# Attention by pairs of query tiles from the first tile on, and a weight conversion without a clamp

## The chip, the core and the metric

The kernel runs on one core of a Trainium2 chip. The metric is the device time of one execution in microseconds (us). The engines are TensorE (PE, with its weight loads as PEld), VectorE (DVE), ScalarE (ACT), GpSimd (POOL) and SyncE (SP), which issues most DMAs. Each engine takes its instructions in the order in which the program gives them, so an instruction that waits holds up everything behind it on its engine.

## What is computed

```python
# 1. local attention: B=4, H=8, S=768, D=64; chunks of 32 queries see 16 keys to
#    the left, 8 to the right, and 8 memory keys
scores = scale * q_c @ k_full.T              # per head and chunk
a = exp(scores - max); a = a / (sum(a) + 1e-9)
out[chunk] = a @ v_full
x = out.transpose(0, 2, 1, 3).reshape(3072, 512)
# 2. gated MLP, weights 512 x 1536 and 1536 x 512, given as float64
g = x @ w_gate
x = (g * sigmoid(g) * (x @ w_val)) @ w_out
# 3. mixture of experts: each token goes to the argmax of 8 experts
out = gate_w * sigmoid(x @ w_output_gate)[e] * (relu(x @ w1[e]) @ w2[e])
```

Queries, keys and values are float32. Products run in a split form: each operand is a high part plus a low part, and three products (high-high, high-low, low-high) are summed.

## The kernel before, in words

**Stages.** The 3072 tokens are eight groups of 384. The attention of group 0 runs first by itself (here "the front"). Then the gated MLP of group 0 runs column by column: the 1536 hidden columns are 12 blocks `f` of 128, and for each block TensorE makes a gate product, a value product and an output product. Between these products the attention of group 1 is fed in, then group 2's while group 1's MLP runs, and so on (`slot` calls `run_pieces`, which issues entries of the list `pieces`). The third stage comes after group 7 and isn't touched here. The order on all engines is that of the Python code, with no scheduler behind it.

**Attention tiles.** A tile is 64 queries (two chunks) of all 8 heads, with 96 keys. `at_T` transposes queries and keys on TensorE; one transpose of queries serves two tiles. For tiles 0 to 13 (`PAIRED` is 14) the queries of a tile are copied into a block-diagonal tile `qbd`: two heads share the 128 rows of the array, each against zeros in the other's half. `at_S` then adds the mask as a product (`identb` times `masks`), makes four products of 128x128 weights, takes the maximum on VectorE and the exponentials on ScalarE. From tile 14 on, `at_S2` makes the scores of two tiles at once from plain queries: sixteen products of 64 rows by 64 columns, four for each pair of heads, each in another quarter of the array. The mask is then added on VectorE (`at_X`). `at_N` divides by the sums (GpSimd up to tile 11), `at_PT` transposes the probabilities, `at_PV` and `at_PV2` multiply them with the values (one tile, two tiles) and split the result into `xh` and `xl`.

**Weights.** While the front and group 0 run, the MLP's weights are converted from float64 in 36 steps of 128x512: `load_w` fetches into one of six staging buffers, `conv_act` starts on ScalarE, `conv_dve` goes on with three VectorE instructions and an addition on GpSimd, and `conv_rest` then asks for a further load. Seven steps are spread over the front, the rest one to a slot. `split_gv` and `split_o` split a block's weights: the high part on ScalarE, the low part on GpSimd. All of this shares the PSUM pool `ps_a` of three buffers with the transposes, the PV products and, from group 1 on, the scores. `LOADS` is the order of the first transfers (w: a weight block, q: queries with their keys, v: values).

Of the kernel before, what the change touches and what calls it, by code (L numbers as in the profile page):

```python
# [21 lines left out]
def tile_chunk_attention_moe_moe2(  # L22
# [324 lines left out]
    def at_S(i, pt=None):  # L347
        t = i % NT
        mi = 1 if t == 0 else (2 if t == NT - 1 else 0)
        mk = masks[:, mi:mi + 1, :].to_broadcast([P, HP, CTXM])  # L350
        fast = i < 15
        qT, kT = qkT[i, 0], qkT[i, 1]
        ps = start_psum(i, ps_o, "o", [P, HP, CTXM])
        if fast:
            nc.tensor.matmul(ps, identb, mk, start=True, stop=False)
        between = iter(()) if pt is None else pt_steps(pt)
        for j in range(HP):
            nc.tensor.matmul(
                ps[:, j, :], qT[:, j, :], kT[:, j, :],
                start=not fast, stop=not fast or j == HP - 1)  # L360
            next(between, None)
        next(between, None)
# [8 lines left out]
        for j in range(HP):  # L371
            nc.scalar.activation(
                out=s[:, j, :], in_=src[:, j, :], func=AF.Exp,
                bias=mx[:, j, :], accum_out=den[:, j, 0:1])
        probs[i] = (s, den)

    def at_S2(i):
        qT = qkT.pop((i, 0))
        kT = [qkT.pop((i + u, 1)) for u in range(2)]
        ps = [ps_a.tile([P, HP, CTXM], F32, tag="a", name="ps_att") for z in range(2)]  # L380
        for j in range(HP):
            for z, u in ((0, 0), (1, 1), (0, 1), (1, 0)):
                d, c = slice(z * D, z * D + D), slice(u * QT, u * QT + QT)
                nc.tensor.matmul(  # L384
                    ps[z][c, j, :], qT[d, j, c], kT[u][d, j, :], start=True, stop=True)
        for z in range(2):
            score[i + z] = ps[z]

    def at_X(i):
        t = i % NT // 2 * 2  # L390
        mi = 3 if t == 0 else (4 if t == NT - 2 else 0)
        mk = masks[:, mi:mi + 1, :].to_broadcast([P, HP, CTXM])
        s = ap2.tile([P, HP, CTXM], F32, tag="s", name="s", bufs=3)
        mx = sm.tile([P, HP, 1], F32, tag="mx", name="mx")
        nc.vector.tensor_tensor(out=s, in0=score.pop(i), in1=mk, op=ALU.add)
        nc.vector.tensor_reduce(out=mx, in_=s, axis=AX.X, op=ALU.max, negate=True)  # L396
        den = dens[i % 3]
        for j in range(HP):
            nc.scalar.activation(  # L399
                out=s[:, j, :], in_=s[:, j, :], func=AF.Exp,  # L400
# [24 lines left out]

    def at_PV(i):
        g, tt = divmod(i, GU)
        if g not in xT:
            xT[g] = (xp.tile([P, KD, GT], F32R, tag="xh", name="xh"),
                     xp.tile([P, KD, GT], F32R, tag="xl", name="xl"))  # L430
        xh, xl = xT[g]
        vt = vals.pop(i)
        u = i % 2
        ps = ps_a.tile([P, HP, QT], F32, tag="a", name="ps_pv")
# [884 lines left out]
```

## Time and profile before

| | us |
|---|---|
| median of 3 runs (lowest to highest) | 1111.65 (1111.19 to 1112.65) |
| the profiled execution's own time | 1112.31 |
| its span, from first to last instruction | 1110.5 |
| busy: PE, PEld | 1075.1 (97%), 966.2 (87%) |
| busy: DVE, ACT, POOL | 585.0 (53%), 594.6 (54%), 630.5 (57%) |
| DMA | 125.73 MB, mean 113 GB/s |

The span leaves 1.8 us of the execution outside it. The shares are means over stages that differ: TensorE is busy nearly all the time after the first 140 us, while VectorE and GpSimd have most of their load in those first 140 us.

### The profile page before, as it was taken

The page shows a single profiled execution, that of the slowest core. Times are in us where ns is not written, and L with a number is a line of the kernel's source. Part 1 is how long each engine was busy: PE and PEld are TensorE (multiplying, and loading weights), DVE is VectorE, ACT ScalarE, POOL GpSimd, SP SyncE. Part 2 cuts the span into 40 slices and gives each one's busy share as a digit, 9 for nine tenths or more (in the row PEclk, how much of TensorE's full clock was granted, in tenths as well). Part 3 has the DMA queues.
Part 4 walks back from the last instruction along what each step waited for, and adds up shares of the span by engine and source line. Part 5 has one row for each costly group of instructions (what it writes and reads, how often), then busy time and mean ns, then how long its engine had stood idle before and what let it go on. Part 6 is the DMA issues. An engine that isn't in the chain of part 4 may idle for free.

```text
span 1110.5 us, 20227 instructions
## 1 busy us (share of the span) xinstructions
PE 1075.1 (97%) x7268; PEld 966.2 (87%) x7268; DVE 585.0 (53%) x1260; ACT 594.6 (54%) x1318; POOL 630.5 (57%) x438
## 2 busy tenths in 40 slices
PE   7899999999999999999999999999999999999994
PEld 5788898998999999899999899899889988888883
DVE  6799944444534543544454353534785444444563
ACT  5588845555555555555555554435544434445551
POOL 4599954654554465564455456565214456667782
PEclk7799999999999999999999999999999999999997
DMA  8887524211211211211121000255329755565774
GB/s 216 211 233 210 140 61 115 67 39 38 59 32 39 68 40 24 56 37 39 39 63 36 22 31 7 89 92 166 126 57 342 242 172 183 181 188 189 223 233 127
DMA packets 204574, 125.73 MB, mean 113 GB/s; under 512 B 110768, under 2 KB 181552, under 8 KB 204466
## 3 DMA queue, kind: packets, MB, share of 16 engines
q1 hardware_dynamic: 199282, 110.70, 36.4%
q0 software_dynamic: 5184, 13.66, 3.6%
q8 instruction: 59, 0.97, 0.4%
q14 instruction: 49, 0.40, 0.1%
HBM read 110.82 MB, written 14.04 MB: 112 GB/s over the span
## 4 chain that ended last, share of the span: by engine, by line
PE 81%; DVE 11%; issue 3%; POOL 2%; ACT 1%; DMA 1%; SPq 0%; POOLq 0%; ACTq 0%; DVEq 0%
PE ps_g L562 32%; PE acc L603 16%; PE g L1071 11%; PE o L1106 11%; PE ps_pv L459 2%; PE ps_t L326 2%; DVE ps_c L229 2%; DVE w L232 2%; DVE ps_c L227 2%; PE ps_att L420 2%; PE ps_att L384 1%; PE ps_x L651 1%; PE a L1057 1%; POOL gvl L184 1%; PE ps_l L659 1%
## 5 line engine op out<-in xcount | busy, mean ns | idle before, releaser
L184 POOL TENSOR_TENSOR gvl<-w,gvh 128x1024 fp32r<-128x1024 f32 x96 | 230.4, 2401 | 98.8 <-ACT gvh L183 97.2
L562 PE MATMUL ps_g<-xh,gvh 128*128 128x384 f32 x768 | 268.5, 350 | 0.6 <-ACT gvh L183 0.6
L562 PE MATMUL ps_g<-xh,gvl 128*128 128x384 f32 x768 | 259.5, 338 | 0.4 <-POOL gvl L184 0.4
L562 PE MATMUL ps_g<-xl,gvh 128*128 128x384 f32 x768 | 259.3, 338 | 0.0
L184 POOL TENSOR_TENSOR ol<-w,oh 128x512 fp32r<-128x512 f32 x96 | 125.6, 1309 | 181.8 <-ACT oh L183 151.8
L603 PE MATMUL acc<-oh,h 128*128 128x512 f32 x576 | 201.0, 403 | 0.0
L575 DVE SCALAR_TENSOR_TENSOR th<-th,ps_g 128x384 f32<-128x384 f32 x96 | 53.1, 553 | 202.8 <-ACT th L570 202.8
L562 PEld LDWEIGHTS ps_g<-xh,gvh 128*128 128x128 f32 x768 | 145.0, 189 | 4.1 <-ACT gvh L183 0.8
L562 PEld LDWEIGHTS ps_g<-xl,gvh 128*128 128x128 f32 x768 | 145.2, 189 | 2.0
L562 PEld LDWEIGHTS ps_g<-xh,gvl 128*128 128x128 f32 x768 | 144.9, 189 | 0.8 <-POOL gvl L184 0.8
L586 ACT CAST h<-th 128x384 fp32r<-128x384 f32 x96 | 49.1, 512 | 155.3 <-DVE th L584 155.3
L603 PEld LDWEIGHTS acc<-oh,h 128*128 128x128 f32 x576 | 108.2, 188 | 26.5 <-issue 3.8
L603 PE MATMUL acc<-ol,h 128*128 128x512 f32 x288 | 113.7, 395 | 0.3 <-POOL ol L184 0.3
L1081 ACT ACTIVATE h<-g 128x256 fp32r<-128x256 f32 (+2 forms) x96 | 36.1, 376 | 141.4 <-PE g L1071 123.4
L183 ACT CAST gvh<-w 128x1024 fp32r<-128x1024 f32 x96 | 100.4, 1047 | 1.6 <-POOL w L235 1.6
L570 ACT ACTIVATE th<-ps_g 128x384 f32<-128x384 f32 x96 | 47.2, 491 | 81.9 <-PE ps_g L562 79.3
L1083 DVE SCALAR_TENSOR_TENSOR h<-g,h 128x256 fp32r<-128x256 f32 (+2 forms) x96 | 39.3, 410 | 94.8 <-ACT hc L1081 41.8
L584 DVE TENSOR_TENSOR th<-th,ps_g 128x384 f32<-128x384 f32 x96 | 53.1, 553 | 68.3 <-PE ps_g L562 66.9
L592 DVE TENSOR_TENSOR h<-th,h 128x384 fp32r<-128x384 f32 x96 | 64.1, 668 | 31.2 <-ACT h L586 31.2
L1106 PE MATMUL o<-wh,h 128*128 128x512 f32 x184 | 65.8, 396 | 0.9 <-DVE h L1083 0.9
L1106 PE MATMUL o<-gvh,h 128*128 128x512 f32 x184 | 66.1, 398 | 0.5 <-DVE h L1083 0.5
L399 ACT ACTIVATE s<-s,mx 128x96 f32<-128x96 f32 x136 | 49.4, 364 | 32.0 <-DVE mx L396 31.9
(254 smaller groups left out, 2275.1 us busy)
## 6 DMA issues: line engine op xcount, KB each, us to landing
w<-in_moe_w_dram SPq DMA_DIRECT2D x120, 256.0 KB
ra<-in_moe_w_dram SPq DMA_DIRECT2D x72, 256.0 KB
kt<-in_k_dram SPq DMA_DIRECT2D x35, 176.0 KB
vt<-in_v_dram SPq DMA_DIRECT2D x35, 176.0 KB
xs<-xr SPq DMA_DIRECT2D x8, 769.5 KB
st<-in_moe_w_gate_dram SPq DMA_DIRECT2D x12, 512.0 KB
st<-in_moe_w_val_dram SPq DMA_DIRECT2D x12, 512.0 KB
st<-in_moe_w_out_dram SPq DMA_DIRECT2D x12, 512.0 KB
```

The costliest lines, as they stand in the source:

```text
L183: nc.scalar.copy(out=hi, in_=src)
L184: lo_eng.tensor_tensor(out=lo, in0=src, in1=hi.bitcast(F32), op=ALU.subtract)
L399: nc.scalar.activation(out=s[:, j, :], in_=s[:, j, :], func=AF.Exp, bias=mx[:, j, :], accum_out=den[:, j, 0:1])
L562: nc.tensor.matmul(ps, a[:, c], x[:, kk, :], start=(n == 0), stop=(n == 3 * KD - 1))
L570: nc.scalar.activation(out=th, in_=ps, func=AF.Tanh, scale=0.5)
L575: nc.vector.scalar_tensor_tensor(out=th, in0=th, scalar=1.0, in1=ps, op0=ALU.add, op1=ALU.mult)
L584: nc.vector.tensor_tensor(out=hh, in0=hh, in1=ps, op=ALU.mult)
L586: nc.scalar.copy(out=h1, in_=hh)
L592: nc.vector.tensor_tensor(out=h2, in0=hh, in1=h1.bitcast(F32), op=ALU.subtract)
L603: nc.tensor.matmul(accs[g][j], a[:, c], w_, start=(f == 0 and n == 0), stop=(f == NF - 1 and n == 2))
L1071: nc.tensor.matmul(ps, wx[:, 0, c * P:(c + 1) * P], xx[:, c, :], start=(i == 0), stop=(i == 3 * KD - 1))
L1106: nc.tensor.matmul(ysd[s][t][0:hx.shape[1]], hx, wx[:, 1], start=(j == 0 and i == 0), stop=(j == NFE - 1 and i == len(passes) - 1))
```

## The change

- Scores go by pairs (`at_S2`) from tile 0 on; `at_S`, `at_PV` and the block-diagonal tiles `qbd` are gone, with their two GpSimd memsets. Queries are copied by one ScalarE instruction for a pair; before it was two, on VectorE in the front and on ScalarE behind it. In the front the mask stays a product; from tile 6 on it is added on VectorE (before: from tile 15 on).
- The pieces of the front are written out by hand in a new order, and `LOADS` with them: queries and keys of four tiles come ahead of most weights and values.
- The conversion loses its first VectorE instruction (the clamp): ScalarE's existing pass multiplies the high word by 2^-112, which moves the exponent as the clamp and the mask did together.
- While group 0 runs, the low part of the output weights (`ol`) is made on VectorE and no more on GpSimd.

```diff
-    LOADS = "w0 q0 q1 q2 w1 v0 v1 q3 w2 q4 w3 w4 v2 w5 q5 v3 v4 v5"
+    LOADS = "q0 q1 w0 q2 q3 w1 v0 v1 w2 q4 q5 w3 v2 v3 w4 v4 v5 w5"
...
-        nc.scalar.activation(out=ps, in_=hi.bitcast(F32), func=AF.Abs)
+        nc.scalar.activation(out=ps, in_=hi.bitcast(F32), func=AF.Abs, scale=REBIAS)
...
         nc.vector.tensor_scalar(
-            out=ps, in0=ps, scalar1=MINF, scalar2=MAXF, op0=ALU.max, op1=ALU.min)
-        nc.vector.tensor_scalar(
-            out=pi, in0=pi, scalar1=3, scalar2=0x3FFFFFFF,
+            out=pi, in0=pi, scalar1=3, scalar2=0x7FFFFFFF,
             op0=ALU.logical_shift_left, op1=ALU.bitwise_and)
...
-    def split_o(f):
+    def split_o(f, lo_eng):
...
-            pair = qbd[i // 2 % 2]
...
+            t = ap2.tile([P, HP, P], F32, tag="qT", name="qT")
+            copy_out(False, t, ps, SCALE)
+            qkT[i, 0] = t
             return
-        t = ap2.tile([P, HP, CTXM], F32, tag="kT", name="kT")
+        t = ap2.tile([P, HP, CTXM], F32, tag="kT", name="kT", bufs=4)
...
+    def at_S2(i):
+        qT = qkT.pop((i, 0))
+        kT = [qkT.pop((i + u, 1)) for u in range(2)]
+        ps = [start_psum(i, ps_o, "o", [P, HP, CTXM]) for z in range(2)]
+        fast = i < GU
         if fast:
-            nc.tensor.matmul(ps, identb, mk, start=True, stop=False)
...
+            mk = pair_mask(i)
+            for z in range(2):
+                nc.tensor.matmul(ps[z], identb, mk, start=True, stop=False)
         for j in range(HP):
...
+            for z, u in ((0, 0), (1, 1), (0, 1), (1, 0)):
+                d, c = slice(z * D, z * D + D), slice(u * QT, u * QT + QT)
+                nc.tensor.matmul(
+                    ps[z][c, j, :], qT[d, j, c], kT[u][d, j, :],
+                    start=not fast, stop=not fast or j == HP - 1)
...
+        yield from convert(0)
         yield at_T, (0, 0)
         yield at_T, (0, 1)
...
+        yield at_T, (1, 1)
+        yield at_S2, (0,)
+        yield at_X, (0,)
+        yield at_T, (2, 0)
+        yield at_T, (2, 1)
+        yield at_X, (1,)
+        yield from convert(1)
+        yield at_N, (0,)
+        yield at_T, (3, 1)
+        yield at_N, (1,)
+        yield at_S2, (2,)
...
+        yield at_X, (4,)
+        yield from convert(4)
+        yield at_PT, (2,)
+        yield at_X, (5,)
+        yield at_PT, (3,)
+        yield from convert(5)
+        yield at_N, (4,)
+        yield at_PV2, (2,)
+        yield at_N, (5,)
+        yield from convert(6)
+        yield at_PT, (4,)
+        yield at_PT, (5,)
+        yield at_PV2, (4,)
...
-                split_o(f)
+                split_o(f, nc.vector if late else nc.gpsimd)
```

**VectorE, the first MLP column of group 0.** Before, from the gate's `th` on (line 575): three instructions to a conversion (L227 is the clamp), with a copy of keys (`kT`), the value's product (L584) and the low part of `h` (L592) between them.

```order
L575 SCALAR_TENSOR_TENSOR th<-th,ps_g 128x384
L227 TENSOR_SCALAR ps_c<-ps_c 128x512
L229 TENSOR_SCALAR ps_c<-ps_c 128x512
L232 SCALAR_TENSOR_TENSOR w<-st,ps_c 128x512
L584 TENSOR_TENSOR th<-th,ps_g 128x384
L315 COPY kT<-ps_t 128x384
L227 TENSOR_SCALAR ps_c<-ps_c 128x512
L229 TENSOR_SCALAR ps_c<-ps_c 128x512
L232 SCALAR_TENSOR_TENSOR w<-st,ps_c 128x512
L592 TENSOR_TENSOR h_665<-th,h_644 128x384
L369 TENSOR_REDUCE mx<-ps_att 128x4
L227 TENSOR_SCALAR ps_c<-ps_c 128x512
```

In the changed program the same stretch, from its line 527 on:

```order
L527 SCALAR_TENSOR_TENSOR th<-th,ps_g 128x384
L178 TENSOR_TENSOR ol<-w,oh 128x512
L307 COPY kT<-ps_t 128x384
L221 TENSOR_SCALAR ps_c<-ps_c 128x512
L224 SCALAR_TENSOR_TENSOR w<-st,ps_c 128x512
L536 TENSOR_TENSOR th<-th,ps_g 128x384
L307 COPY kT<-ps_t 128x384
L221 TENSOR_SCALAR ps_c<-ps_c 128x512
L224 SCALAR_TENSOR_TENSOR w<-st,ps_c 128x512
L544 TENSOR_TENSOR h_667<-th,h_647 128x384
L221 TENSOR_SCALAR ps_c<-ps_c 128x512
L224 SCALAR_TENSOR_TENSOR w<-st,ps_c 128x512
```

A conversion has two instructions, and `ol`, which was GpSimd's, stands behind the gate's `th` in every column.

**VectorE, where a pair of PV products is copied out in group 0.** Before, with the tile's `xh` and `xl`:

```order
L575 SCALAR_TENSOR_TENSOR th<-th,ps_g 128x384
L315 CAST xh<-ps_pv 128x4x128
L468 TENSOR_TENSOR xl<-ps_pv,xh 128x4x128
L227 TENSOR_SCALAR ps_c<-ps_c 128x512
L229 TENSOR_SCALAR ps_c<-ps_c 128x512
L232 SCALAR_TENSOR_TENSOR w<-st,ps_c 128x512
L584 TENSOR_TENSOR th<-th,ps_g 128x384
```

After:

```order
L178 TENSOR_TENSOR ol<-w,oh 128x512
L307 CAST xh<-ps_pv 128x4x128
L407 TENSOR_TENSOR xl<-ps_pv,xh 128x4x128
L360 TENSOR_TENSOR s<-ps_att,masks 128x384
L362 TENSOR_REDUCE mx<-s 128x4
L221 TENSOR_SCALAR ps_c<-ps_c 128x512
L224 SCALAR_TENSOR_TENSOR w<-st,ps_c 128x512
```

Behind `xl` now come the mask addition (L360) and maximum (L362) of the next pair's scores, whose products TensorE makes after the PV products; `ol` stands in front.

**ScalarE, the start of the front.** Before, from the first conversion step (L218, L219); L372 are the four exponentials of a tile, L423 copies transposed probabilities:

```order
L218 ACTIVATE ps_c<-st 128x512
L219 ACTIVATE st<-st 128x512
L372 ACTIVATE s,den_104<-ps_att,mx 128x96 x4
L218 ACTIVATE ps_c<-st 128x512
L219 ACTIVATE st<-st 128x512
L372 ACTIVATE s,den_105<-ps_att,mx 128x96 x4
L218 ACTIVATE ps_c<-st 128x512
L219 ACTIVATE st<-st 128x512
L423 COPY pT<-ps_att 96x512
L372 ACTIVATE s,den_106<-ps_att,mx 128x96 x4
```

After, where L365 are the exponentials and L305 copies the queries of a pair:

```order
L212 ACTIVATE ps_c<-st 128x512
L213 ACTIVATE st<-st 128x512
L305 ACTIVATE qT<-ps_t 128x512
L365 ACTIVATE s,den_104<-ps_att,mx 128x96 x4
L305 ACTIVATE qT<-ps_t 128x512
L365 ACTIVATE s,den_105<-ps_att,mx 128x96 x4
L212 ACTIVATE ps_c<-st 128x512
L213 ACTIVATE st<-st 128x512
L365 ACTIVATE s,den_106<-ps_att,mx 128x96 x4
L212 ACTIVATE ps_c<-st 128x512
```

The queries' copies have come to ScalarE, the first of them behind the conversion of w0, and the exponentials of tiles 0 and 1 now stand ahead of the second conversion.

## Rows read from the trace of the kernel before

**Rows 1.** Windows (us, then busy PE, PEld, DVE, ACT, POOL, clock, DMA, GB/s).

```profile
47.40:134.00 86.60, 79.06 (x514) 69.90 (x513) 82.90 (x145) 73.15 (x169) 78.07 (x57) 1.00 0.74 206
134.00:154.70 20.70, 20.70 (x141) 19.15 (x141) 12.12 (x21) 9.86 (x24) 13.06 (x9) 1.00 0.21 53
154.70:245.70 91.00, 89.82 (x673) 82.22 (x673) 40.63 (x89) 50.00 (x121) 47.31 (x27) 1.00 0.29 72
```

**Rows 2.** Timeline of VectorE from 47.36 us: start, duration, instruction.

```profile
47.36 0.56 DVE L315 COPY kT<-ps_t 128x384 f32<-128x384 f32 x1 [6.10 <-PE ps_t L326]
47.84 0.69 DVE L227 TENSOR_SCALAR ps_c<-ps_c 128x512 f32<-128x512 f32 x1
48.56 0.70 DVE L229 TENSOR_SCALAR ps_c<-ps_c 128x512 int32<-128x512 int32 x1
49.29 0.69 DVE L232 SCALAR_TENSOR_TENSOR w<-st,ps_c 128x512 int32<-128x512 int32 x1
49.90 0.55 DVE L575 SCALAR_TENSOR_TENSOR th<-th,ps_g 128x384 f32<-128x384 f32 x1
```

**Rows 3.** Groups by line, 47.4 to 134: busy us, mean ns.

```profile
L227 DVE TENSOR_SCALAR ps_c<-ps_c 128x512 f32<-128x512 f32 x29 | 19.9, 686 | 0.0
...
L592 DVE TENSOR_TENSOR h<-th,h 128x384 fp32r<-128x384 f32 x9 | 6.0, 662 | 0.0
```

**Rows 4.** Timeline of VectorE: the end of group 0.

```profile
154.72 0.69 DVE L632 TENSOR_SCALAR xr<-acc 128x512 f32<-128x512 f32 x1 [0.40 <-PE acc L603]
```

**Rows 5.** Timeline of TensorE: scores of one tile at 61.07, of two at 351.11.

```profile
61.07 0.34 PE L355 MATMUL ps_att<-masks,identb 128*128 128x384 bf16 x1
...
62.05 0.42 PE L562 MATMUL ps_g<-xh,gvh 128*128 128x384 f32 x1
...
351.11 0.89 PE L384 MATMUL ps_att<-kT,qbd 64*64 64x96 f32 x32
351.93 0.50 PE L603 MATMUL acc<-oh,h 128*128 128x512 f32 x1
```

**Rows 6.** The mask addition on VectorE: ns min/median/max.

```profile
L395 DVE TENSOR_TENSOR s<-ps_att,masks x34: 545/548/551, 167.4 to 663.5; 128x384 f32<-128x384 f32 x34
```

**Rows 7.** Low parts made on VectorE in the third stage: ns min/median/max.

```profile
L1007 DVE TENSOR_TENSOR gvl<-w,gvh x36: 669/691/2756, 789.1 to 1068.0; 128x512 fp32r<-128x512 f32 x36
L1007 DVE TENSOR_TENSOR wl<-w,wh x36: 669/691/1360, 796.6 to 1072.8; 128x512 fp32r<-128x512 f32 x36
```

**Rows 8.** Timeline of the front, SP and ScalarE.

```profile
0.81 0.44 SPq L204 DMA_DIRECT2D st<-in_moe_w_gate_dram  x1
...
4.85 0.63 ACT L218 ACTIVATE ps_c<-st 128x512 f32<-128x512 f32 x1 [2.44 <-DMA st<-in_moe_w_gate_dram]
...
5.41 0.64 ACT L219 ACTIVATE st<-st 128x512 int32<-128x512 uint32 x1
...
10.86 0.34 ACT L372 ACTIVATE s<-ps_att,mx 128x96 f32<-128x96 f32 x1 [4.81 <-DVE mx L369]
```

**Rows 9.** Timeline of the end of the front.

```profile
36.39 0.83 POOL L410 TENSOR_TENSOR s<-s,rec 128x384 f32<-128x384 f32 x1 [1.24 <-ACT ps_c L218]
...
37.27 1.09 PE L420 MATMUL ps_att<-ident,s 128*96 128x128 f32 x4 [1.22 <-POOL s L410]
...
38.37 1.97 PE L437 MATMUL ps_pv<-pT,first 96*64 96x64 f32 x32
38.40 0.58 ACT L423 COPY pT<-ps_att 96x512 f32<-96x512 f32 x1 [1.10 <-PE ps_att L420]
...
40.01 4.67 POOL L184 TENSOR_TENSOR gvl<-w,gvh 128x1024 fp32r<-128x1024 f32 x2 [0.36 <-ACT gvh L183]
...
42.41 0.69 PE L562 MATMUL ps_g<-xh,gvl 128*128 128x384 f32 x1 [0.41 <-POOL gvl L184]
...
46.02 0.49 ACT L570 ACTIVATE th<-ps_g 128x384 f32<-128x384 f32 x1 [5.15 <-PE ps_g L562]
```

**Rows 10.** The chain of waits: the exponentials of tile 0.

```profile
10.86 1.41 ACT s L372 x8
```

**Rows 11.** Windows of the front.

```profile
10.00:38.40 28.40, 23.91 (x165) 20.16 (x164) 24.35 (x52) 17.66 (x66) 14.54 (x27) 0.62 0.93 239
38.40:46.70 8.30, 7.28 (x49) 6.52 (x50) 2.29 (x6) 2.96 (x4) 5.91 (x3) 0.50 0.78 194
```

**Rows 12.** Timeline of TensorE: a pair of PV products in group 0.

```profile
119.76 1.15 PE L459 MATMUL ps_pv<-pT,vt 96*64 96x64 f32 x32 [0.31 <-ACT kT L317]
```

**Rows 13.** The chain of waits: one product of a column, 134 to 160.

```profile
136.56 2.11 PE ps_g L562 x12
138.66 2.10 PE acc L603 x9
```

More of the change, by code (lines that the diff above doesn't have):

```diff
@@ L345, in at_T, with pair_mask, at_X @@
         qkT[i, 1] = t
[L347 to L353, printed above, removed]
+    def pair_mask(i):
+        t = i % NT // 2 * 2
+        mi = 3 if t == 0 else (4 if t == NT - 2 else 0)
+        return masks[:, mi:mi + 1, :].to_broadcast([P, HP, CTXM])
+    def at_S2(i):
[3 more added lines that the diff above has]
+        fast = i < GU
         if fast:
-            nc.tensor.matmul(ps, identb, mk, start=True, stop=False)
-        between = iter(()) if pt is None else pt_steps(pt)
+            mk = pair_mask(i)
+            for z in range(2):
+                nc.tensor.matmul(ps[z], identb, mk, start=True, stop=False)
         for j in range(HP):
[L358 to L362, printed above, removed]
+            for z, u in ((0, 0), (1, 1), (0, 1), (1, 0)):
[3 more added lines that the diff above has]
+                    start=not fast, stop=not fast or j == HP - 1)
+        for z in range(2):
+            score[i + z] = ps[z]
+    def at_X(i):
         s = ap2.tile([P, HP, CTXM], F32, tag="s", name="s", bufs=3)
         mx = sm.tile([P, HP, 1], F32, tag="mx", name="mx")
-        src = ps
-        if not fast:
-            nc.vector.tensor_tensor(out=s, in0=src, in1=mk, op=ALU.add)
+        src = score.pop(i)
+        if i >= GU:
+            nc.vector.tensor_tensor(out=s, in0=src, in1=pair_mask(i), op=ALU.add)
             src = s
@@ L373, in at_S @@
                 out=s[:, j, :], in_=src[:, j, :], func=AF.Exp,
[L374 to L400, printed above, removed]
                 bias=mx[:, j, :], accum_out=den[:, j, 0:1])
@@ L412, in at_PT @@
     def at_PT(i):
-        for _ in pt_steps(i):
-            pass
-    def pt_steps(i):
         p = probs.pop(i)[0]
@@ L424, in pt_steps @@
         pT[i] = t
[L426 to L434, printed above, removed]
-        for h in range(H):
-            z = h % 2
-            nc.tensor.matmul(
-                ps[z * D:z * D + D, h // 2, :], vt[:, h, :],
-                pT[i][:, h // 2, z * QT:z * QT + QT] if i < PAIRED
-                else pT[i - u + z][:, h // 2, u * QT:u * QT + QT],
-                start=True, stop=True)
-        dst = (slice(None), slice(None), slice(tt * QT, (tt + 1) * QT))
-        if i + 3 >= GU:
-            load_v(i + 3)
-        copy_out(i < 2 * GU, xh[dst], ps)
-        nc.vector.tensor_tensor(out=xl[dst], in0=ps, in1=xh[dst].bitcast(F32), op=ALU.subtract)
     def at_PV2(i):
@@ new lines, in attention_pieces @@
+        yield at_S2, (0,)
[8 more added lines that the diff above has]
+        yield at_S2, (2,)
+        yield at_X, (2,)
+        yield from convert(2)
+        yield at_PT, (0,)
+        yield at_T, (4, 0)
+        yield at_X, (3,)
+        yield at_PT, (1,)
+        yield at_T, (4, 1)
+        yield from convert(3)
+        yield at_N, (2,)
@@ L501, in attention_pieces @@
+        yield at_T, (5, 1)
+        yield at_PV2, (0,)
+        yield at_N, (3,)
+        yield at_S2, (4,)
+        yield at_X, (4,)
[11 more added lines that the diff above has]
+        yield at_PV2, (4,)
         yield at_T, (GU, 0)
         yield at_T, (GU, 1)
-        for n in range(GU, PAIRED):
-            yield at_T, (n + 1, 0)
-            yield at_T, (n + 1, 1)
-            if n % 2 == 0 and n - 4 >= GU:
-                yield at_PV2, (n - 4,)
-            yield at_S, (n,)
-            if n - 2 >= GU:
-                yield at_PT, (n - 2,)
-            if n - 1 >= GU:
-                yield at_N, (n - 1,)
@@ L513, in attention_pieces @@
[L513 to L519 removed]
+        yield at_T, (GU + 1, 1)
+        for n in range(GU, NTT + 2, 2):
+            if n > GU:
                 yield at_PT, (n - 2,)
@@ L1147, in tile_chunk_attention_moe_moe2 @@
                 load_w(*divmod(z, 3))
-        run_pieces(12)
+        run_pieces(pieces.index((at_S2, (2,))))
         setup_routing()
```

77 lines of the change are left out of this document (21 added, 56 removed).

## Prediction

> **What bounds the kernel now.** I first looked where the change lies: the front, and group 0 of the MLP, up to the copy of group 0's sums at 154.72 us [rows 4]. Behind that point the code of groups 1 to 7 and of the third stage is the same, apart from an order of pieces that group 2 had already. Group 1 took 91.0 us with TensorE busy for 89.8 of it at the full clock [rows 1], so nothing off TensorE matters there.
>
> The windows split the beginning in three. From 47.4 to 134 us VectorE is busy 82.9 of 86.6 us; TensorE (79.1), GpSimd (78.1) and ScalarE (73.2) come behind it [rows 1]. The reader is to see in the timeline [rows 2] that VectorE's instructions stand without a gap, one starting as the last one ends: copy, clamp, shift, merge, silu. From 134 to 154.7 TensorE is busy all the time [rows 1]: the conversions are over. So VectorE sets the time from 47.4 to 134, TensorE after that.
>
> Ahead of 47.4 lies the front. There VectorE is busy 24.4 of 28.4 us between 10 and 38.4, TensorE 23.9, at a mean clock of 0.62 [rows 11]; it is a chain of latencies that VectorE paces. It ends with the last copy of probabilities on ScalarE (38.40, 0.58 long), the split of the first weights on GpSimd (40.01) and TensorE going on at 42.41 behind it [rows 9]. VectorE then has nothing to do until 47.36, 6.1 us [rows 2].
>
> **The change part by part, group 0.** The sum is made against the profiled execution's 1112.3 us, which is 0.66 above the median.
>
> *The clamp.* It takes 686 ns, 29 times in the stretch [rows 3]; from its start to the next instruction's it is 0.72 us (47.84 to 48.56) [rows 2]. 29 x 0.72 = 20.9 us come off VectorE. ScalarE's pass stays the same instruction with a factor; I price that at nothing.
>
> *The idle time before 47.36.* VectorE waits there for a copy of keys whose transposes stand behind the first gate product. In the new order only queries come at that place, and they go to ScalarE. The seventh conversion's two instructions (0.73 + 0.61, [rows 2]) therefore run in the gap: -1.3 us.
>
> *`ol` on VectorE.* The same operation and shape stands in the third stage: median 0.69 us, but up to 2.76 [rows 7]. In the stretch the low part of `h`, also a subtraction of two SBUF tiles, has a mean of 662 ns for 384 columns [rows 3], where a 384-column instruction that reads PSUM takes 0.55 [rows 2, 6]. So there is some waiting beside a busy GpSimd. I take 0.76 for each of the 10 that fall in the stretch: +7.6 us; bounds 0.6 and 2.76. The Trainium skill, "GPSIMD Engine Reference" (Specifications), states that GpSimd's SBUF interface is shared with VectorE and contended by VectorE instructions with two SBUF inputs. The trace agrees: the long ones are of that kind. By that rule an edit that adds ten such instructions beside GpSimd costs more than their bare 0.69 us, or 6.9 in all.
>
> *The mask on VectorE.* Eight tiles (6 to 13) at 548 ns [rows 6], 0.48 from start to start, as for the copy of keys, which is of that size (47.36 to 47.84, [rows 2]): +3.8 us.
>
> *Waits that come with the pairs.* `at_S2` takes two buffers of `ps_a`, which has three; one is held by the conversion in flight and one by the PV products just made. So the second half of the scores waits until `xl` is copied out on VectorE, and VectorE's next instruction is the mask addition of these same scores. It stands idle for the sixteen products, 0.82 us [rows 5], and some 0.1 of handover, four times: +3.6. Lower bound 0; upper bound 2.5 each, if VectorE also waits for the PV products (1.15 us, [rows 12]) with its queue empty.
>
> *What costs nothing here.* On TensorE a tile took 0.98 us for mask and scores (61.07 to 62.05), a pair will take 0.82 [rows 5]: 4 x (1.96 - 0.82) = 4.6 us less, which hides behind VectorE as long as VectorE is the bound. GpSimd loses ten `ol`, and ScalarE four copies of queries; neither ended a wait that counts. If VectorE stops being the bound, TensorE is next (rival B).
>
> **The front.** Now the chain is longer, as pairs wait for both tiles. Its steps at 1.2 GHz, in which most of the front ran:
> - Start. w0 landed 4.04 us after its request at 0.81 [rows 8]. Now q0 and the keys of two tiles (0.6 MB) are ahead of its 0.5 MB, which at 239 GB/s [rows 11] moves its landing to about 7.4 us (estimate: 0.8, 1.9 of start-up, 4.7 of transfer). ScalarE, in order, then converts (1.2, two passes, [rows 8]), copies the queries (0.6); the second tile's keys get their PSUM buffer only then: transposes 0.9, copy 0.6, scores 1.6 (double of 0.82), maximum 0.6. The exponentials of tile 0 start at 12.9; before, at 10.86.
> - To the exponentials of tile 2: VectorE has keys, maximum, conversion, sums, keys (4.6), then scores 1.6 and a maximum: 6.8.
> - To those of tile 4: ScalarE has two tiles' exponentials (1.41 each, [rows 10]), a conversion, two copies of probabilities and one of queries (5.8); then PV products 1.97 [rows 9], two masks 1.1, scores and maximum: 11.0.
> - To the last copy of probabilities: 5.2 of ScalarE, then PV 2.0, `xh` and `xl` 1.3, the sums 0.3, the division 0.83, the transposes 1.09, the copy 0.58 [rows 9]: 11.3, since the division of tile 5 stands behind the copies of the PV products.
>
> That is 42.0 us. With TensorE's pieces halved it would be 35.9. At the mean clock of 0.62 (a quarter of the time at 2.4 GHz) it is 40.5, against 38.98 before: +1.5. Bounds -3.1 and +3.0. The conversions' clamps and the block-diagonal copies that leave the front are inside these steps: they no longer set it.
>
> **Sum.** -20.9 - 1.3 + 7.6 + 3.8 + 3.6 + 1.5 = -5.7: 1106.6 for the profiled execution, 1106.0 against the median.
>
> **The rivals.**
> - *B: TensorE becomes the bound of group 0.* The waits of the pairs vanish in VectorE's reserves and nothing holds TensorE. Its floor: group 1's 91.0, two further products of 2.1 [rows 13] (the gate and value of group 1's first column lie ahead of the copy), 1.8 for the first product at the half clock [rows 11], some 2 for the first pair of group 1: 99 from 42.41, so 141.4 instead of 154.7. With the front's 1.5 that is -11.8: 1100. For it: VectorE's sum falls below TensorE's. Against it: VectorE, TensorE, ScalarE and GpSimd would all be above four fifths busy, each in order.
> - *C: the gain is given back.* The four pairs cost 2.0 each (+4.4), and the front stays at 1.2 GHz throughout (+1.5): 1111.9, no difference. For it: the front spends most of its time at that clock already [rows 11].
> - *D: slower.* GpSimd holds VectorE up at every `ol`. The price decides: without `ol` the sum is -13.3, so it is even at 1.33 us each and slower by over 0.2% at 1.55. At 2.0 it is +6.7: 1118. For it: the maxima of 1.36 and 2.76 [rows 7]. Against it: the medians of 0.69 in a stage where GpSimd does the same subtractions.
>
> **How the numbers follow.** Main case 0.60, with a range of its own from 1102 to 1109.5 (waits from nothing to 1.8 each, the front from -2 to +2.5). B 0.16, C 0.16, D 0.08. The likeliest gives 1106. 0.2%, about what a measurement of this kernel can tell from no change, is 2.2 us: 1109.4 to 1113.9. The main case lies almost wholly below that, so faster 0.76, same 0.16, slower 0.08. From 1099.5 to 1111.5 is left out less than half of B and C and all of D, under 2 in 10.
>
> **What the profile after would show.** The clamp right: two instructions to a conversion, 1.34 us from start to start. Group 0: its sums copied near 149 (154.72 less 5.7); VectorE still densest between 47 and 130, with gaps of about 0.9 at each mask addition that follows `xl`. `ol` near 0.76 in the mean. The front: the exponentials of tile 0 near 12.9, the last copy of probabilities near 40. From there to the end the same 956 us as before; if these differ, I have overlooked something in the later groups. The prediction is wrong if the mean of `ol` passes 1.3, if TensorE rather than VectorE is without gaps in group 0, or if the front ends more than 3 us from where I put it.

## The result, and the profile after

The changed kernel takes 1122.3 us (1121.6 to 1122.6), the kernel before 1112.15 in the same comparison: ratio 1.0091, 95% interval 1.0077 to 1.0105. It is 10 us slower, where 1106.0 was forecast with a range up to 1111.5: the forecast was wrong in its sign. The profiled execution took 1122.49.

Timeline of VectorE in the kernel after, the ends of groups 0 and 1:

```profile
165.71 0.69 DVE L584 TENSOR_SCALAR xr<-acc 128x512 f32<-128x512 f32 x1
...
256.37 0.69 DVE L584 TENSOR_SCALAR xr<-acc 128x512 f32<-128x512 f32 x1 [0.84 <-PE acc L555]
```

Group 0 ends at 165.71 where it ended at 154.72 [rows 4]: +11.0, the whole loss. From there to the end the profiled executions take 956.8 us, and 957.6 before. Windows of the kernel after (columns as in [rows 1]):

```profile
10.00:38.40 28.40, 20.09 (x214) 15.84 (x214) 15.59 (x35) 18.28 (x67) 13.52 (x25) 0.68 0.96 239
50.00:130.00 80.00, 66.84 (x468) 57.29 (x467) 63.40 (x110) 56.11 (x133) 54.49 (x39) 0.91 0.69 192
165.70:256.40 90.70, 90.70 (x681) 82.81 (x681) 40.50 (x90) 51.05 (x124) 47.64 (x27) 1.00 0.30 79
```

And of the kernel before, in the middle stretch:

```profile
50.00:130.00 80.00, 73.82 (x482) 65.48 (x483) 77.22 (x136) 67.74 (x159) 74.07 (x55) 1.00 0.75 213
```

The columns after the length of a window are the busy time of PE, PEld, DVE, ACT and POOL. Every engine got emptier: VectorE fell from 77 to 63 of 80 us, but TensorE from 74 to 67 as well, and its mean granted clock from 1.00 to 0.91. No engine is nearly full any more; they wait for one another. The waits of VectorE from 46 to 165 us say where (engine, what waits, for what: us in all, times, longest):

```profile
DVE ol L178 <- ACT oh L177: 11.3, 10, 1.6
DVE th L527 <- ACT th L522: 8.6, 9, 3.0
DVE s L360 <- PE ps_att L349: 3.5, 2, 1.7
```

The first can't occur in the kernel before, where `ol` is GpSimd's, and it was not in the forecast. One of the ten, in VectorE's timeline:

```profile
85.82 0.56 DVE L527 SCALAR_TENSOR_TENSOR th<-th,ps_g 128x384 f32<-128x384 f32 x1 [0.40 <-ACT th L522]
88.01 1.63 DVE L178 TENSOR_TENSOR ol<-w,oh 128x512 fp32r<-128x512 f32 x1 [1.64 <-ACT oh L177]
89.57 0.68 DVE L307 CAST xh<-ps_pv 128x512 fp32r<-128x512 f32 x1
90.28 0.69 DVE L407 TENSOR_TENSOR xl<-ps_pv,xh 128x512 fp32r<-128x512 f32 x1
92.69 0.56 DVE L360 TENSOR_TENSOR s<-ps_att,masks 128x384 f32<-128x384 f32 x1 [1.73 <-PE ps_att L349]
93.29 0.55 DVE L362 TENSOR_REDUCE mx<-s 128x4 f32<-128x384 f32 x1
```

in ScalarE's at the same time:

```profile
85.69 0.58 ACT L305 ACTIVATE qT<-ps_t 128x512 f32<-128x512 f32 x1
86.16 0.65 ACT L212 ACTIVATE ps_c<-st 128x512 f32<-128x512 f32 x1
86.75 0.67 ACT L213 ACTIVATE st<-st 128x512 int32<-128x512 uint32 x1
87.32 0.60 ACT L177 CAST oh<-w 128x512 fp32r<-128x512 f32 x1
93.88 0.38 ACT L365 ACTIVATE s<-s,mx 128x96 f32<-128x96 f32 x1 [5.95 <-DVE mx L362]
```

and in TensorE's, with a window of the 2 us behind its wait:

```profile
91.11 1.55 PE L349 MATMUL ps_att<-kT,qT 64*64 64x96 f32 x30 [3.61 <-DVE xl L407]
```

```profile
91.10:93.20 2.10, 2.09 (x32) 1.78 (x33) 0.51 (x1) 0.00 (x0) 0.00 (x0) 0.50 1.04 255
```

VectorE reaches `ol` and stands 1.64 us, since ScalarE has a copy of queries and a conversion ahead of `oh`. Then `ol` takes 1.63. Behind it stand `xh` and `xl`. The second half of the pair's scores on TensorE waits 3.61 us for `xl` and then runs at a granted clock of 0.50, the lower level (1.2 GHz). The mask and the maximum wait for these scores, and the exponentials for the maximum; ScalarE, with its next conversion behind them, is idle 5.95 us.

**What `ol` takes.** Groups by line from 49.4 to 150 us in the kernel after (busy us, mean ns | idle ahead):

```profile
L178 DVE TENSOR_TENSOR ol<-w,oh 128x512 fp32r<-128x512 f32 x11 | 13.2, 1202 | 12.8 <-ACT oh L177 11.3 <-issue 1.5
```

These `ol` take 1.20 us in the mean, not 0.76. Four of them in VectorE's timeline,

```profile
52.10 0.69 DVE L178 TENSOR_TENSOR ol<-w,oh 128x512 fp32r<-128x512 f32 x1 [1.60 <-ACT oh L177]
...
60.29 1.10 DVE L178 TENSOR_TENSOR ol<-w,oh 128x512 fp32r<-128x512 f32 x1 [1.18 <-ACT oh L177]
...
88.01 1.63 DVE L178 TENSOR_TENSOR ol<-w,oh 128x512 fp32r<-128x512 f32 x1 [1.64 <-ACT oh L177]
...
119.47 1.64 DVE L178 TENSOR_TENSOR ol<-w,oh 128x512 fp32r<-128x512 f32 x1 [1.64 <-ACT oh L177]
```

and what GpSimd does at the times of the last three (at 52.10 it does nothing):

```profile
58.46 2.39 POOL L178 TENSOR_TENSOR gvl<-w,gvh 128x1024 fp32r<-128x1024 f32 x1
60.80 1.76 POOL L227 TENSOR_TENSOR w<-w,st 128x512 int32<-128x512 int32 x1
...
87.82 1.28 POOL L227 TENSOR_TENSOR w<-w,st 128x512 int32<-128x512 int32 x1
...
119.27 1.28 POOL L227 TENSOR_TENSOR w<-w,st 128x512 int32<-128x512 int32 x1
```

With GpSimd idle, `ol` takes 0.69 us. GpSimd's instructions end at 60.85, 89.10 and 120.55; the three `ol` end 0.54, 0.54 and 0.56 later, and so do the other eight of group 0 that meet a GpSimd instruction (0.54 to 0.56). So the rows read as if `ol` did not run slowly, but stood until GpSimd's instruction is over. The `w` that GpSimd starts at 60.80 stands in turn, 1.76 us in place of 1.28. The Trainium skill, "SBUF — State Buffer" (SBUF: two separate sides), states just that: the pair of ports that VectorE and GpSimd share is an exclusive lock, and of a VectorE instruction with two SBUF inputs and a GpSimd instruction that reads SBUF the one that starts first holds it for its whole length. The trace agrees, with the ends above.

**The front** of the kernel after, timeline of all engines:

```profile
8.77 0.62 ACT L212 ACTIVATE ps_c<-st 128x512 f32<-128x512 f32 x1 [6.36 <-DMA st<-in_moe_w_gate_dram]
...
9.99 0.60 ACT L305 ACTIVATE qT<-ps_t 128x512 f32<-128x512 f32 x1
...
10.64 0.42 PE L318 MATMUL ps_t<-ident,first 96*128 96x96 f32 x1 [4.42 <-ACT qT L305]
...
14.38 0.34 ACT L365 ACTIVATE s<-ps_att,mx 128x96 f32<-128x96 f32 x1 [3.79 <-DVE mx L362]
...
41.52 0.58 ACT L384 COPY pT<-ps_att 96x512 f32<-96x512 f32 x1 [2.27 <-PE ps_att L382]
...
49.43 0.49 ACT L522 ACTIVATE th<-ps_g 128x384 f32<-128x384 f32 x1 [5.44 <-PE ps_g L514]
```

The first exponentials come at 14.38 (forecast 12.9; before 10.86 [rows 8]), the last copy of probabilities ends at 42.10 (forecast 40.5; before 38.98), the first gate's tanh starts at 49.43 (before 46.02 [rows 9]): +3.4, where +1.5 was forecast. The start is late as forecast, by conversion 0 standing ahead of the queries' copy on ScalarE, but w0 landed at 8.77, not 7.4.

### The profile page after: what moved, and what is told of

It is laid out like the page before. It is cut to its first block, busy times and chain, and to the rows that moved or that the text cites. A ratio compares the mean times of both kernels' runs of the same rounds, so it can differ in the third digit from the quotient of the medians.

```text
span 1120.7 us, 20388 instructions
## 1 busy us (share of the span) xinstructions
PE 1071.5 (96%) x7372; PEld 960.0 (86%) x7372; DVE 574.1 (51%) x1232; ACT 592.4 (53%) x1317; POOL 616.8 (55%) x424
## 4 chain that ended last, share of the span: by engine, by line
PE 77%; issue 5%; DVE 5%; ACT 5%; POOL 4%; SPq 3%; DMA 1%; POOLq 0%; DVEq 0%; ACTq 0%
PE ps_g L514 29%; PE acc L555 15%; PE g L1023 12%; PE o L1058 11%; PE ps_pv L398 2%; SPq L267 2%; PE ps_t L318 2%; PE ps_att L382 2%; POOL gvl L178 2%; PE ps_att L349 1%; PE ps_x L603 1%; PE a L1009 1%; ACT st L213 1%; ACT ps_c L212 1%; ACT gvh L177 1%
## 5 line engine op out<-in xcount | busy, mean ns | idle before, releaser
L178 POOL TENSOR_TENSOR ol<-w,oh 128x512 fp32r<-128x512 f32 x84 | 110.4, 1314 | 171.6 <-ACT oh L177 143.9
L555 PE MATMUL acc<-oh,h 128*128 128x512 f32 x576 | 203.9, 408 | 0.0
L365 ACT ACTIVATE s<-s,mx 128x96 f32<-128x96 f32 x168 | 61.0, 364 | 51.0 <-DVE mx L362 51.0
L1035 DVE SCALAR_TENSOR_TENSOR h<-g,h 128x256 fp32r<-128x256 f32 (+2 forms) x96 | 39.4, 410 | 93.3 <-ACT hc L1033 47.4
L522 ACT ACTIVATE th<-ps_g 128x384 f32<-128x384 f32 x96 | 47.0, 489 | 75.7 <-PE ps_g L514 75.3
L227 POOL TENSOR_TENSOR w<-w,st 128x512 int32<-128x512 int32 x36 | 51.7, 1436 | 43.0 <-ACT s L365 18.6
```

The costliest lines, as they stand in the source:

```text
L178: lo_eng.tensor_tensor(out=lo, in0=src, in1=hi.bitcast(F32), op=ALU.subtract)
L227: nc.gpsimd.tensor_tensor(out=wi, in0=wi, in1=lo, op=ALU.add)
L365: nc.scalar.activation(out=s[:, j, :], in_=src[:, j, :], func=AF.Exp, bias=mx[:, j, :], accum_out=den[:, j, 0:1])
L555: nc.tensor.matmul(accs[g][j], a[:, c], w_, start=(f == 0 and n == 0), stop=(f == NF - 1 and n == 2))
```

## Experiments

My first theory (A) was that the pairs in group 0 lose the time, by stalls at their scores. Rival B: `ol` stands behind `oh`. Rival C: the clamp was worth nothing, since VectorE was not the bound. The runs, each against the kernel before on the same chip ("us" is the ratio's difference x 1112; the interval of a row is 1.0 to 1.7 us to either side, so that of a difference of two rows is 1.4 to 2.3):

| run | median us | ratio, 95% interval | us |
|---|---|---|---|
| e1 no clamp | 1109.5 | 0.9978 (0.9966 to 0.9989) | -2.4 |
| e2 `ol` | 1129.4 | 1.0156 (1.0142 to 1.0170) | +17.3 |
| e3 pairs, tiles 6 to 13 | 1120.9 | 1.0078 (1.0065 to 1.0092) | +8.7 |
| e4 front | 1117.4 | 1.0048 (1.0034 to 1.0062) | +5.3 |
| after | 1122.3 | 1.0091 (1.0077 to 1.0105) | +10.1 |
| e5 after, `ol` on GpSimd | 1114.0 | 1.0020 (1.0011 to 1.0029) | +2.2 |
| e6 no clamp, `ol` | 1115.2 | 1.0030 (1.0018 to 1.0042) | +3.3 |
| e7 no clamp, `ol` later | 1105.6 | 0.9949 (0.9935 to 0.9962) | -5.7 |
| e8 after, scores split off | 1121.6 | 1.0083 (1.0069 to 1.0097) | +9.2 |
| e9 after, `ol` later | 1115.1 | 1.0027 (1.0017 to 1.0037) | +3.0 |
| e10 = e9, conversion 0 later | 1114.5 | 1.0024 (1.0015 to 1.0033) | +2.7 |
| e11 = e7 with pairs | 1111.7 | 0.9993 (0.9984 to 1.0002) | -0.8 |
| e12 = e10, front reordered | 1112.3 | 0.9999 (0.9990 to 1.0008) | -0.1 |
| e13 = e11, mask by matmul | 1108.1 | 0.9969 (0.9958 to 0.9981) | -3.4 |
| e14 = e11, scores ahead | 1131.9 | 1.0176 (1.0162 to 1.0190) | +19.6 |
| e15 clamp, `ol` later | 1123.0 | 1.0098 (1.0082 to 1.0113) | +10.9 |
| e16 = e13 and e14 | 1132.1 | 1.0183 (1.0169 to 1.0197) | +20.4 |
| e17 = e6, `oh` earlier | 1109.5 | 0.9979 (0.9970 to 0.9988) | -2.3 |
| e18 = e12, mask by matmul | 1109.0 | 0.9975 (0.9965 to 0.9984) | -2.8 |

**Each part alone (e1 to e4).** e1 and e2 take their lines of the change's diff and nothing else. e3 keeps the front of before and lets the loop by pairs begin with tile 6:

```diff
-    PAIRED = 2 * GU + 2
+    PAIRED = GU
```

e4 is the reverse: order, loads and pairs of the new front, tiles 6 to 13 as before.

> The kernel before with the clamp alone left out (29 instructions of 0.69 us on VectorE gone). Theory A (the loss of the change comes from pairs of tiles in group 0, whose score matmuls wait for two accumulators of PSUM, and behind them the exps and conversions on ScalarE): VectorE bounds group 0 of the kernel before, so this part by itself gains 10 to 20 us, 1092 to 1102. Rival B (the loss comes from `ol` on VectorE, which stands there behind `oh` of ScalarE): the same, 1092 to 1102. Rival C (VectorE was not what bounded group 0, the freed time is only idle time elsewhere): under 3 us of gain, 1109 to 1112.

> The kernel before with `ol` of group 0 alone moved from GpSimd to VectorE. Theory A: about its duration, 10 x 0.76 = +7.6 us at most, since VectorE is the full engine there: 1115 to 1120. Rival B: duration and wait, 7.6 + 11.3 (the idle time of VectorE ahead of ol in the kernel after) = +12 to +19, 1124 to 1131. Rival C: within 2 us of before.

> The kernel before, front and all, with tiles 6 to 13 alone by pairs, as the tiles from 14 on are in it (mask added on VectorE, both scores at once). Theory A: two stalls of TensorE of some 3.6 us, the half clock after them and the exps' wait of 19 us on ScalarE come with it: +6 to +13 us, 1118 to 1125. Rival B: the 7 mask adds and nothing else, less the faster score matmuls: +1 to +4, 1113 to 1116. Rival C: no more than 1 us either way.

> The kernel before with the front of the kernel after alone (tiles 0 to 5 by pairs, in its order and with its order of loads; clamp, ol and tiles 6 to 13 as before). All theories price the front by the gate's tanh in the two traces, 49.43 against 46.02: +3.4 us, 1114 to 1116. If the time lost in the front is given back in group 0 (its first stretch has idle time of VectorE and TensorE to spare), it is under 1.5 us: 1111 to 1113; if the late last conversions of the front hold up group 0 as well, it is over 5 us: 1117 or more.

The sum is +28.9, the whole +10.1: the parts do not add. The clamp alone gives 2.4 of the 20.9 us forecast: C's range, against A and B, which both expected 1092 to 1102. Windows of e1:

```profile
50.00:130.00 80.00, 74.16 (x478) 65.98 (x478) 67.58 (x107) 68.38 (x160) 75.41 (x56) 0.98 0.74 209
...
70.00:90.00 20.00, 17.47 (x127) 15.40 (x126) 16.96 (x26) 17.37 (x37) 20.00 (x15) 1.00 0.83 243
```

VectorE fell to 67.6, but GpSimd is at 75.4, in one window 20.00 of 20, and TensorE at 74. The next engines stand right behind VectorE, so its 20 us are worth little alone. `ol` alone costs over twice its price in the sum and lies in B's range, but not by B's wait: VectorE waits 2.0 us for `oh` in e2, where B had taken 11.3. The twelve `ol` themselves are 16.3 us long (groups by line, 46 to 166 us of e2):

```profile
L184 DVE TENSOR_TENSOR ol<-w,oh 128x512 fp32r<-128x512 f32 x12 | 16.3, 1362 | 5.3 <-ACT oh L183 2.0 <-POOL w L235 1.8 <-POOL gvl L184 1.5
```

The pairs cost what A said, though not by A's two stalls of 3.6 us: TensorE waits 2.6 us in all for `xl` in e3. The front costs more than the +3.4 of the traces: 5.3, the case in which it holds up group 0 as well.

**Two parts together, and the place of `ol` (e5 to e8).** e5 puts `ol` of the kernel after back on GpSimd; e6 is before with no clamp and `ol`; e7 leaves `oh` in `split_o` and issues `ol` on VectorE in a function of its own, later:

```diff
                 slot(3 * f + 1)
                 if late:
                     m1_h1(f)
+                    split_ol(f)
```

e8 cuts the piece of the kernel after that holds the PV products and the next scores:

```diff
-                yield at_PVS, (n - 2,)
+                yield at_PV2, (n - 2,)
+                yield at_T, (n + 2, 1)
+                yield at_SX, (n,)
```

> The kernel after with `ol` of group 0 back on GpSimd, all else as it is. Theory D (the parts do not add: by itself each of clamp, ol, pairs and front gave -2.5, +17.4, +8.9 and +5.4, which is +29.3 and not the +10.2 of the whole; without the clamp the engine that is full next is GpSimd, which ol on VectorE relieves, so the two belong together): with ol back, GpSimd has its 20 us of work more and is full, 1122 to 1130. Rival E (ol costs in the kernel after what it costs by itself, since VectorE stands behind oh of ScalarE whatever else is done; something else, pairs with the clamp gone, makes up the 19 us): 1103 to 1110.

> The kernel before with the clamp left out and `ol` of group 0 on VectorE, both and nothing else. Theory D: the clamp's 0.69 us and ol's 0.76 us change places on VectorE, GpSimd loses 20 us, and the kernel is faster than with either part: 1098 to 1108. Rival E: ol's wait stays, 1116 to 1126 (the clamp's -2.5 beside ol's +17.4 would be 1127).

> As the run before with `ol` on VectorE issued one slot later, after the multiplication of h, when oh has long been copied. Theory D: the wait for oh was a small part of it, within 3 us of the run before (1098 to 1108). Rival E: the wait goes and with it most of ol's cost; by the durations alone 10 x 0.76 us on VectorE, which has over 20 us free without the clamp: 1100 to 1109, and 10 us or more under the run before.

> The kernel after with the score pair of tiles 8 to 13 taken out of the piece of the value products: the transpose of the next k stands between them, so that the copy of xl has its time before the second score's accumulator is wanted. Theory A (the two stalls of 3.6 us of TensorE at S2 and the exps' wait behind them): 4 to 8 us faster than the kernel after, 1114 to 1118. Rival: the third accumulator is then held by that transpose, and its copy stands behind xl: no change within 2 us of 1122, or slower.

D fell by e5: with `ol` on GpSimd the kernel after is 7.9 us faster, not slower; E's 1103 to 1110 is missed too (1114.0). e6 lies just under E's range and far above D's. e7 against e6 tells most: the same instructions, `ol` one slot later, 9.0 us. With it the clamp's removal pays at last. e8 changed 0.9, within the intervals. TensorE's wait for `xl` is gone there, but others have come (VectorE waits 4.6 us for a copy of keys): the stall that A named was not by itself the loss.

**The kernel after, repaired step by step, and pairs in e7 (e9 to e12).** e9 is the later `ol` in the kernel after, e11 the pairs of e3 in e7. e10 and e12 change the front:

```diff
-        yield from convert(0)
         yield at_T, (0, 0)
...
         yield at_X, (0,)
+        yield from convert(0)
...
-        yield at_PV2, (0,)
-        yield at_N, (3,)
         yield at_S2, (4,)
         yield at_X, (4,)
+        yield at_N, (3,)
+        yield at_PV2, (0,)
...
-        yield at_PV2, (2,)
         yield at_N, (5,)
+        yield at_PV2, (2,)
```

(the first two places are e10, the others come with e12)

> The kernel after with `ol` on VectorE issued one slot later, after the multiplication of h, as in the run that gave 1105.56. Theory F (the step that failed is the place of ol: VectorE stands behind oh of ScalarE, and everything behind ol on VectorE with it; the front and the pairs cost 2 to 5 us beside): 1106 to 1111, some 12 to 16 us under the kernel after. Rival G (in the kernel after it is also that GpSimd and VectorE work against each other while ol runs on VectorE, which the place doesn't change): 1112 to 1118.

> As the run before, with conversion 0 on ScalarE moved from the first place of the front to behind the exps of tile 0. In the trace of after the second k transpose waits 4.42 us for the copy of qT, which stands on ScalarE behind conversion 0, and that waits for w0 to land at 8.77. If this is what made the front late: the scores of the front's first pair start 2 to 4 us earlier and the run is 2 to 4 us faster than e9. Rival (the front's chain is set later, by PV2 and the last loads): under 1 us.

> The kernel of the run that gave 1105.56 (front of before, no clamp, ol one slot later) with tiles 6 to 13 by pairs; it is e9 with the front of before. Theory A (pairs in group 0 cost by stalls, +9 alone): 1109 to 1115. Rival (pairs cost only while VectorE is full with the clamp; without it the mask adds and waits have room, and TensorE's shorter scores gain): 1101 to 1105.

> As e10, with the third score pair of the front ahead of the first value products, and the normalization of tile 5 ahead of the second value products (in the trace of after VectorE stands idle 3.12 us ahead of the copy of xh, with the sum for tile 5 behind it). If that is on the front's chain: 1.5 to 4 us faster than e10. Rival (loads of v and the three accumulators set it): within 1 us.

e9 gives 7.1 us back, and TensorE's waits for `xl` shrink with it, so `ol` ahead of `xl` had made them long (waits of TensorE from 46 to 166 us, the kernel after and then e9):

```profile
PE ps_att L349 <- DVE xl L407: 7.2, 2, 3.6
```

```profile
PE ps_att L356 <- DVE xl L414: 2.6, 2, 1.3
```

F's 1106 to 1111 is missed; e9 lies where G put it, but G's reason (the lock) it doesn't show, as pairs and front cost as much. e10: 0.3, no difference. Its ScalarE starts the first exponentials 3.9 us earlier than e9's (10.23 against 14.11) and the first gate's tanh 1.0 (48.02 against 49.03), so the late start was mostly not on the front's chain. Timelines of ScalarE, e9 and then e10:

```profile
14.11 0.34 ACT L372 ACTIVATE s<-ps_att,mx 128x96 f32<-128x96 f32 x1 [3.79 <-DVE mx L369]
...
49.03 0.49 ACT L529 ACTIVATE th<-ps_g 128x384 f32<-128x384 f32 x1 [5.56 <-PE ps_g L521]
```

```profile
10.23 0.34 ACT L372 ACTIVATE s<-ps_att,mx 128x96 f32<-128x96 f32 x1 [3.16 <-DVE mx L369]
...
48.02 0.49 ACT L529 ACTIVATE th<-ps_g 128x384 f32<-128x384 f32 x1 [5.41 <-PE ps_g L521]
```

e12: 2.8, as expected; the sum for tile 5 behind `xh`, or the scores behind the first PV products, were on that chain (the two were not parted). e11: pairs still cost 4.9 with VectorE relieved.

**Why pairs cost, and what the clamp is worth (e13 to e16).** e13 adds the mask of tiles 6 to 13 by a matmul ahead of the scores; e14 issues `at_S2(n)` ahead of `at_PT(n - 2)`; e16 is both; e15 is e7 with the clamp put back.

> The run e11 (1111.65: front of before, no clamp, ol one slot later, tiles 6 to 13 by pairs) with the mask of tiles 6 to 13 put in by a matmul ahead of the scores, as the single tiles of before have it, in place of the addition on VectorE. Theory H (the pairs cost by the addition of 0.55 us between scores and exps, 8 times, while ScalarE waits): 4 to 6 us faster than e11, 1105 to 1108. Theory I (they cost by their order and by two accumulators at once): within 1.5 us of e11, 1110 to 1113.

> The run e11 with the scores of the pairs 8, 10 and 12 two pieces ahead of their exps: ahead of the transposes of the last pair's probabilities, and no longer in one piece with the value products. Theory I: ScalarE no longer stands behind scores just issued (it waited 16.9 us in all for the maxima in e11, 7.8 in the single-tile run), 3 to 6 us faster than e11, 1105 to 1109. Theory H: within 1.5 us of e11.

> The kernel before with `ol` of group 0 on VectorE one slot later and nothing else: the run that gave 1105.56 with the clamp put back. Theory J (VectorE is full in group 0 of before, so ol costs it its own time when the clamp stays, and the clamp is worth that much there): 8 to 16 us over 1105.56, 1114 to 1121. Rival (TensorE is nearly full in all of these and sets the end, the clamp is worth its -2.5 of the front and no more): 1106 to 1110.

> The edits of e13 and e14 together. If H and I each hold in part: 1101 to 1106, and under 1105 it would beat the single-tile run. If neither: within 1.5 us of 1111.65.

e13: the mask additions cost 2.7 of the pairs' 4.9 us, between H (4 to 6) and I (under 1.5). ScalarE's waits for the maxima, 16.9 us in e11 and 7.8 in e7 (49 to 150 us), are still 13.2 in e13. e14 and e16 tell nothing on theory I: a rule that counts group 0's pieces took tile 8's exponentials into the front, and TensorE stood there for a load, before the first gate (timeline of e14):

```profile
49.31 1.09 PE L330 MATMUL ps_t<-ident,qt 128*128 128x128 f32 x4 [7.32 <-DMA qt<-in_q_dram]
```

e15 confirms J's direction; its 16.6 us lie above J's 8 to 16. Windows of e15 and then of e7:

```profile
50.00:130.00 80.00, 67.75 (x429) 60.58 (x430) 76.42 (x128) 61.08 (x141) 55.75 (x39) 0.96 0.73 203
```

```profile
50.00:130.00 80.00, 75.67 (x500) 68.24 (x500) 73.70 (x121) 68.47 (x166) 66.33 (x46) 1.00 0.79 218
```

With the clamp VectorE is the one engine that is nearly full (76.4); without it TensorE has risen from 67.8 to 75.7. There the clamp is worth 16.6 us.

**The wait or the place, and the whole repaired (e17, e18).** e17 copies `oh` ahead of slot 3f and leaves `ol` where the change puts it; e18 is e12 with the mask of e13.

> The run e6 (1115.2: front and single tiles of before, no clamp, ol on VectorE where the change puts it) with oh copied on ScalarE a slot earlier, ahead of the pieces of slot 3f, so that ol has nothing to wait for. Theory K (the wait for oh, 11.3 us in all in e6, is the price of the place): 8 to 11 us faster than e6, 1104 to 1108, as e7. Rival (it is the work of ol itself ahead of the multiplication of h, 0.7 to 1.6 us in each of 12 columns): 1111 to 1115.

> The run e12 (1112.28: the kernel after with ol one slot later, conversion 0 and the order of the front changed) with the mask of tiles 6 to 13 put in by a matmul as in e13. If the mask is worth here what it was in e13 (3.55 us): 1107 to 1110, 12 to 15 us under the kernel after and faster than before. Rival (the front's late start sets the stretch here, and the mask is hidden): 1111 to 1113.

e17 lies between K and its rival: taking the wait for `oh` away gives 5.7 of the 9.0 us of place. All its `ol` in group 0 (ns min/median/max):

```profile
L258 DVE TENSOR_TENSOR ol<-w,oh x12: 678/1968/2429, 47.4 to 143.5; 128x512 fp32r<-128x512 f32 x12
```

It waits for nothing, but takes 1.97 us in the median: at this place GpSimd is mostly in `gvl` of the next column. The twelve `ol` of e6, e17 and e7, and then of the kernel after and e9, with the idle time ahead of them (46 to 166 us):

```profile
L183 DVE TENSOR_TENSOR ol<-w,oh 128x512 fp32r<-128x512 f32 x12 | 12.7, 1058 | 14.4 <-ACT oh L182 11.3 <-POOL gvl L183 1.6 <-issue 1.5
L258 DVE TENSOR_TENSOR ol<-w,oh 128x512 fp32r<-128x512 f32 x12 | 21.5, 1792 | 0.1
L261 DVE TENSOR_TENSOR ol<-w,oh 128x512 fp32r<-128x512 f32 x12 | 18.4, 1534 | 0.0
```

```profile
L178 DVE TENSOR_TENSOR ol<-w,oh 128x512 fp32r<-128x512 f32 x12 | 15.3, 1277 | 12.8 <-ACT oh L177 11.3 <-issue 1.5
L256 DVE TENSOR_TENSOR ol<-w,oh 128x512 fp32r<-128x512 f32 x12 | 14.5, 1212 | 0.0
```

The length alone orders the runs wrongly: e6 has the shortest `ol` of the first three and is the slowest. Length and idle time together are 27.1, 21.6 and 18.4 us, in steps of 5.5 and 3.2, and the runs differ by 5.7 and 3.3. So the lock at this place would account for e17's other 3.3 us; that is argued from these rows, for `ol` also stands ahead of the multiplication of `h` there (the rival), and no run parts the two. Nor is it a rule: from the kernel after to e9 the same sum falls by 13.6 and the run by 7.1. e18: with the four repairs the change is 12.9 us faster than as it stood, and faster than before.

## Why the prediction was wrong

1. **The clamp and `ol` on VectorE: the step that failed.** Forecast -20.9 and +7.6, together -13.3; e6 has these two parts and nothing else and gives +3.3. That is 16.6 us, more than the whole error of 15.8. The runs, us against before:

   | | with the clamp | without it |
   |---|---|---|
   | `ol` on GpSimd | 0 | -2.4 (e1) |
   | `ol` on VectorE, where the change puts it | +17.3 (e2) | +3.3 (e6) |
   | `ol` on VectorE, one slot later | +10.9 (e15) | -5.7 (e7) |

   The clamp is worth 2.4, 14.0 or 16.6, and `ol` at its place costs 17.3 or 5.7: neither has a price of its own, and the sum added the two as if they had. It failed in two places. (a) *"I take 0.76 for each"* priced `ol` by its duration. In the kernel after it is 1.20 in the mean, with 12.8 us of idle time ahead of eleven. I had not asked what `ol` waits for, nor what waits behind it. Its place costs 9.0 of the 16.6 us (e7 against e6): 5.7 of that went with the wait (e17). (b) *"So VectorE sets the time from 47.4 to 134"* was taken as if all that comes off VectorE were gain; the other engines of [rows 1] stood too close. The relief of GpSimd was put at nothing (*"neither ended a wait that counts"*), yet without the clamp GpSimd is the fullest (e1), and `ol` moved off it to a place without a wait gains 3.3 (e7 against e1). Even e7 stops at -5.7, 7.6 short of the forecast for its parts, with TensorE at 75.7 and VectorE at 73.7 of 80; that these 7.6 went to the near-fullness of these two is read from the windows, and no run isolates it.
2. **Mask, waits of the pairs, front.** Forecast 3.8, 3.6, 1.5 and the -1.3 of the gap, together +7.6; between e6 and the kernel after it is +6.8, but with the later `ol` (e7 to e9) 8.7. That the sum is near is in part luck, for the terms are not: the mask measured 2.7 (e13 against e11, e18 against e12) for 3.8 (eight tiles: before, it is added on VectorE from tile 14 on, not 15), and the front 3.8 (e9 against e11) for 1.5; its order makes 2.8 of that (e12). The rest of the pairs is 2.3 (e13 against e7, hardly clear of the intervals), as forecast (3.6 - 1.3), but the waits came otherwise in the kernel after: two of 1.7 us in place of four of 0.9, so that 3.5 in all is luck as well.
3. **The rivals.** D had the sign, the place and the mechanism that `ol` meets GpSimd, but its price of 1.55 as duration was not reached: 1.20, and a wait that it did not have. B did not come: TensorE idled more, not less. C did not come: the front's mean granted clock was 0.68, not 0.5, and VectorE's waits at the pairs were 3.5 us in all, not 2.0 at each of four.
4. **What held:** the two-instruction conversion, the seventh conversion in the gap (45.49 and 46.22, ahead of the first `th` at 49.95), and the time behind group 0 (956.8 us). None of the signs of being wrong showed: `ol` at 1.20 (1.28 over all twelve) stayed under 1.3, TensorE was not without gaps, and the front ended 1.6 us from its forecast. The sign that did show was the copy of group 0's sums, at 165.71 in place of 149.

Open: the pairs' last 2.3 us, as e14 was no test of them, and which of e12's two moves counts.

## What to carry to other kernels

Price an instruction that is moved to another engine by three things: its duration beside what runs there at that time, its wait for operands at its new place in that engine's order, and what is queued behind it. Put the consumer of another engine's copy a slot later, and read again. Here four engines were over 80% busy, and work taken off the fullest alone was worth about the distance to the next (2.4 us, where 3.1 lay between VectorE and GpSimd). So price removals and moves together, as one sum per engine, and take the largest as the least time possible, with the waits on top. The best version here keeps single tiles, drops the clamp and places `ol` later: 1105.6 us (e7).

## What the runs showed of the hardware

In the kernel after, a subtraction of two SBUF tiles on VectorE, 0.69 us with GpSimd idle, ended 0.54 to 0.56 us after the GpSimd instruction in whose time it was issued, and GpSimd's next one then stood 0.48 us for it (1.76 against 1.28). `gvl` on GpSimd, being there first, kept its 2.4 us. So the duration of such an instruction is not a fixed figure: mostly it is the rest of what GpSimd has begun and some 0.55 us. It can be more: one `ol` of e7 (at 82.85 us) let two further GpSimd instructions go first and took 2.71 us.
